# ScalarE's unused statistics outputs go to a scratch tile of 4-byte elements instead of the normalised tile of 2-byte elements

## The chip, the cores and the metric

One NeuronCore of one Trainium2 chip runs the kernel. The metric is the device time of one execution in microseconds (us); where several runs are compared, the median is quoted. The profile's own clock, the span, runs from the first to the last instruction and is about 1.8 us shorter than the device time (242.4 against 244.21 us for the profiled run of before). Of the engines, TensorE multiplies matrices, VectorE, ScalarE and GpSimd (POOL in the profile) do the elementwise work and the statistics, and SyncE issues most of the loads; a load "lands" when its data has arrived. The "granted clock" is TensorE's clock as a share of its full one, as the profile gives it. "Before" and "after" are the kernel without and with the change.

## The reference

It is one block of a diffusion transformer, with B=2, N=256 tokens, D=1152, two heads and an MLP of width F=4608, all in bf16:

```python
mod = (_silu(c) @ w_mod).reshape(B, 6, 1, D)
shift_a, scale_a, gate_a, shift_m, scale_m, gate_m = [mod[:, i] for i in range(6)]
h = _layernorm(x, axis=-1) * (1 + scale_a) + shift_a
qkv = (h @ wqkv).reshape(B, N, 3, H, Dh)
# ... q, k, v; softmax(q k^T / sqrt(Dh)) v, times wo
x = x + gate_a * a
h2 = _layernorm(x, axis=-1) * (1 + scale_m) + shift_m
m = _gelu(h2 @ w_fc1) @ w_fc2
return x + gate_m * m
```

Only the first layer norm matters here. Its mean and variance are taken per token over D.

## The kernel before

The 512 tokens lie in four token tiles of 128. The loads of x are issued first, on SyncE's queue, in the order 0, 1, 3, 2. Weight loads follow on the same queue: pieces of `w_scale_a` in turn with rows of `w_k`.

VectorE takes the statistics of tiles 1 and 3 with its own instructions. ScalarE takes those of tiles 0 and 2, each with two passes, Identity and Square. Each pass also gives the sum of its outputs (the trace has a read of an accumulator, 186 ns, after each), and only that sum is wanted; the call takes an output tile for the elements all the same. Before, they go into the tile that VectorE later fills with the normalised values.

```python
xns = [work.tile([P, D], BF16, name="xn", tag="xn", bufs=4) for _ in range(NT)]
# ...
def act_stats(t):
    for f, dst in ((ACT.Identity, dsum), (ACT.Square, dsq)):
        nc.scalar.activation(
            xns[t][:], x_sb[:, t, :], f, bias=x_sb[:, t, 0:1], scale=-1.0,
            accum_out=dst[:, t:t + 1],
        )
# ... the order in which the start is issued (cut):
warm(8, pwarm)                       # filler matmuls, meant to keep TensorE's clock up
act_stats(0)
act_stats(2)
for j in range(NPD):
    stats_piece(1, j)                # VectorE, tile 1
# ... variance and 1/std of tiles 0, 1 and 3
norm1(1, 0, CUT)                     # VectorE writes xns[1], xns[0]
norm1(0, 0, CUT)
pt_a = transpose_x([0, 1], BT[0])    # TensorE transposes xns[0], xns[1]
# ...
act_var(2)                           # needs the last ScalarE pass
nc.vector.tensor_scalar_mul(hT0[:, 0, 0:N], pt_a[:, 0, :], pm0[:, 0, 0:1])
# ... then matmuls with w_k, with scale_group(6, 8) and the like between:
def scale_group(k0, k1, tile_of=aux_tile):     # one block of scale_a = w_scale_a^T silu(c)
    # ...
            nc.tensor.matmul(
                pm[:, j - k0, :], w_scale_a[:, k, j * P:(j + 1) * P], sT[:, k, 0:B], # ...
            )
```

Much later the softmax's tile and then the residual x1 use one slot of scratch memory (the tag decides the slot):

```python
soft = act.tile([P, 4 * n_s * N], BF16, name="soft", tag="x1")
# ...
x1 = act.tile([P, NT, D], FP32, name="x1", tag="x1")
```

## Time and profile before

| | before |
|---|---|
| time, three runs | 243.87, 244.08, 244.36 us |
| span of the profiled run | 242.4 us |
| TensorE busy | 98% of the span |
| ScalarE busy | 25% of the span |
| the four statistics passes | 1254 to 1256 ns each |

First the profile page of before, part 1: busy time of each engine, its share of the span, and its count of instructions.

```profile
PE 237.1 (98%) x1701; PEld 145.0 (60%) x1701; DVE 91.4 (38%) x193; ACT 59.6 (25%) x120; POOL 28.9 (12%) x48
```

The chain of waits of before, in order of time (start, duration, what), from 8.5 us on:

```profile
8.53 2.51 SPq L104
11.04 0.04 issue
11.08 8.69 DMA w_scale_a<-in_w_mod_dram
19.77 0.05 issue
19.82 0.60 PE pm L245 x18
```

It is read backwards from the last instruction. From 19.82 us on nothing but TensorE holds the chain until the last output. Up to there this trace puts a weight load on it, and no ScalarE work. The `w_scale_a` piece in question is the fourth of five, and its matmuls belong to the blocks 6 and 7. I call it "the fourth piece". TensorE's own rows of the timeline show the wait (in brackets the idle time before an instruction and what ended it):

```profile
17.73 1.46 PE L278 MATMUL pk<-big,w_k 128*128 128x512 bf16 x6
19.82 0.60 PE L245 MATMUL pm<-sT,w_scale_a 128*128 128x2 bf16 x18 [0.64 <-DMA w_scale_a<-in_w_mod_dram]
```

The timeline of before, ScalarE only (start, duration, instruction, then in brackets the idle time before it and what ended it):

```profile
3.66 1.25 ACT L204 ACTIVATE xn<-x_sb 128x1152 bf16<-128x1152 bf16 x1
4.82 0.19 ACT L204 ACTIVATION_READ_ACCUMULATOR xn<-x_sb 128x1 f32 x1
5.04 1.25 ACT L204 ACTIVATE xn<-x_sb 128x1152 bf16<-128x1152 bf16 x1
...
7.18 1.26 ACT L204 ACTIVATE xn<-x_sb 128x1152 bf16<-128x1152 bf16 x1 [0.79 <-DMA x_sb<-in_x_dram]
...
8.56 1.26 ACT L204 ACTIVATE xn<-x_sb 128x1152 bf16<-128x1152 bf16 x1
```

From one pass to the next of the same tile is 1.38 us, which holds the pass and the read of its sum. The third pass waits for its token tile to arrive, not for a buffer. And the waits of before (who, for whom: us in total, times, longest):

```profile
PE pm L245 <- DMA w_scale_a<-in_w_mod_dram: 0.6, 1, 0.6
PEld L262 <- ACT xn L204: 0.6, 1, 0.6
```

The second line names ScalarE as what the first transposes waited for.

### The profile page before, as it was taken

The numbers are of one execution on the slowest core, as the hardware profiler recorded it, in microseconds if no ns is written. First come the engines' busy times: TensorE is split into PE (matmuls) and PEld (weight loads), VectorE is DVE, ScalarE is ACT, GpSimd is POOL, SyncE is SP. The second block draws the span as 40 slices with busy tenths as digits, with TensorE's granted clock in tenths as the row PEclk, the third lists the DMA queues.
The fourth block names the chain that finished last, engine by engine and source line by source line (L and its number), as shares of the span: only waits on it lengthen the run. The fifth ranks groups of instructions, "written<-read, shape, count | busy, mean of one in ns | idle before, by whom it ended". The sixth has DMA issues, their size and how long they took to land.

```text
span 242.4 us, 3999 instructions
## 1 busy us (share of the span) xinstructions
PE 237.1 (98%) x1701; PEld 145.0 (60%) x1701; DVE 91.4 (38%) x193; ACT 59.6 (25%) x120; POOL 28.9 (12%) x48
## 2 busy tenths in 40 slices
PE   8998999999999999999999999999999999999994
PEld 5675454465567665888854444444656656655674
DVE  4742442318416578831002999960010000000001
ACT  6622332307215032671422233322000000000000
POOL 2400000001400333200000000001121111111111
PEclk9999999999999999999999999999999999999999
DMA  6999999996499999239999999999300000000000
GB/s 184 325 317 318 376 366 391 390 392 236 107 314 398 388 374 145 40 62 351 390 391 392 342 327 290 271 326 286 97 16 16 20 16 16 20 16 17 29 22 16
DMA packets 48781, 53.29 MB, mean 220 GB/s; under 512 B 9587, under 2 KB 36475, under 8 KB 48763
## 3 DMA queue, kind: packets, MB, share of 16 engines
q1 hardware_dynamic: 41312, 50.14, 62.2%
q10 hardware_dynamic: 6939, 1.71, 5.1%
q0 software_dynamic: 512, 1.19, 1.8%
q8 instruction: 13, 0.21, 0.4%
q14 instruction: 5, 0.04, 0.1%
HBM read 50.14 MB, written 1.19 MB: 212 GB/s over the span
## 4 chain that ended last, share of the span: by engine, by line
PE 91%; SPq 4%; DMA 4%; issue 0%; DVE 0%; DVEq 0%
PE pacc L732 29%; PE pacc L788 29%; PE pacc L679 7%; PE pacc L588 7%; PE pq L510 7%; DMA w_scale_a<-in_w_mod_dram 4%; SPq L104 3%; PE pk L307 2%; PE pk L278 2%; PE pa L628 2%; PE ps_s L545 2%; PE pn L405 2%; SPq L86 1%; SPq L107 1%; PE pg L487 0%; PE pm L245 0%
## 5 line engine op out<-in xcount | busy, mean ns | idle before, releaser
L732 PE MATMUL pacc<-hT,w_f 128*128 128x256 bf16 (+1 forms) x432 | 70.5, 326 | 0.0
L788 PE MATMUL pacc<-w_f,gT 128*128 128x384 bf16 (+2 forms) x468 | 70.5, 314 | 0.0
L788 PEld LDWEIGHTS <-gT 128*128 128x128 bf16 x468 | 44.4, 98 | 26.3
L732 PEld LDWEIGHTS <-w_f 128*128 128x128 bf16 x432 | 42.2, 98 | 27.6
L794 DVE TENSOR_TENSOR tmp<-pacc,gate 128x384 f32<-128x384 f32 (+2 forms) x13 | 6.9, 527 | 65.6 <-PE pacc L788 57.2
L764 ACT ACTIVATE gT<-pacc 128x512 bf16<-128x512 f32 x24 | 14.3, 597 | 32.6 <-PE pacc L732 32.6
L458 DVE SCALAR_TENSOR_TENSOR part<-w_gate_m,s,part 128x1152 f32<-128x1152 bf16 x16 | 21.4, 1412 | 0.0
L796 POOL TENSOR_TENSOR o_sb<-tmp,x 128x384 bf16<-128x384 f32 (+1 forms) x12 | 11.7, 972 | 54.1 <-DVE tmp L794 54.1
L679 PE MATMUL pacc<-w_o,big 128*128 128x384 bf16 x108 | 17.9, 326 | 0.0
L510 PE MATMUL pq<-hT,w_q 128*128 128x512 bf16 x81 | 17.8, 379 | 0.0
L588 PE MATMUL pacc<-w_v,hT 128*128 128x384 bf16 x108 | 17.7, 326 | 0.0
L588 PEld LDWEIGHTS <-hT 128*128 128x128 bf16 x108 | 10.5, 98 | 7.1 <-issue 0.3
L679 PEld LDWEIGHTS <-big 128*128 128x128 bf16 x108 | 10.4, 98 | 7.2 <-issue 0.4
L510 PEld LDWEIGHTS <-w_q 128*128 128x128 bf16 x81 | 7.8, 97 | 9.5
L278 PE MATMUL pk<-big,w_k 128*128 128x256 bf16 (+1 forms) x72 | 13.2, 326 | 0.0
L685 POOL TENSOR_TENSOR x<-tmp,x_sb 128x384 f32<-128x384 f32 x8 | 7.3, 913 | 27.1 <-DMA w_scale_m<-in_w_mod_dram 15.2
L456 DVE TENSOR_SCALAR part<-w_gate_m,s 128x1152 f32<-128x1152 bf16 x2 | 1.6, 818 | 22.1 <-DMA w_gate_m<-in_w_mod_dram 22.1
L480 POOL DMA_DIRECT2D gates_dram<-nat_v x2 | 1.1, 536 | 67.7 <-DVE nat_v L478 67.7
L278 PEld LDWEIGHTS <-w_k 128*128 128x128 bf16 x72 | 6.7, 98 | 3.7 <-issue 0.3
L753 ACT ACTIVATE gT<-pacc 128x512 bf16<-128x512 f32 x12 | 6.5, 598 | 9.1 <-PE pacc L732 9.1
L173 PE MATMUL pwarm<-zeros 128*128 128x256 f32 x20 | 7.2, 527 | 1.2 <-DVE eps_t L93 1.2
L501 POOL DMA_DIRECT2D gates_dram<-nat x4 | 2.3, 586 | 50.6 <-DVE nat L498 49.9
(101 smaller groups left out, 165.9 us busy)
## 6 DMA issues: line engine op xcount, KB each, us to landing
w_f<-in_w_fc_dram SPq DMA_DIRECT2D x12, 864.0 KB, 14.6
w_f<-in_w_fc_dram SPq DMA_DIRECT2D x3, 1728.0 KB, 7.8
w_f<-in_w_fc_dram SPq DMA_DIRECT2D x2, 2592.0 KB, 17.2
w_gate_a<-in_w_mod_dram SPq DMA_DIRECT2D x3, 864.0 KB, 11.8
w_v<-in_wqkv_dram SPq DMA_DIRECT2D x3, 864.0 KB, 13.9
w_o<-in_wo_dram SPq DMA_DIRECT2D x3, 864.0 KB, 14.0
w_shift_m<-in_w_mod_dram SPq DMA_DIRECT2D x3, 864.0 KB, 8.6
w_scale_m<-in_w_mod_dram SPq DMA_DIRECT2D x3, 864.0 KB, 13.4
```

Source lines behind the costliest of these rows:

```text
L104: nc.sync.dma_start(w_k[:, k0:k1, c0:c1], wqkv_v[:, k0:k1, D + c0:D + c1])
L173: nc.tensor.matmul(dst[:, 0:T // 2], zeros32[:, 0:P], zeros32, start=True, stop=True)
L278: nc.tensor.matmul(pk[m][:, c0:c1], w_k[:, k, m * P:(m + 1) * P], hT0[:, k, c0:c1], start=(k == 0 and c0 == 0), stop=(k == KD - 1), skip_g ...
L458: nc.vector.scalar_tensor_tensor(part[:, b, :], wg[:, k, :], s32[:, k, b:b + 1], part[:, b, :], op0=ALU.mult, op1=ALU.add,)
L510: nc.tensor.matmul(pq[m][:], w_q[:, k, m * P:(m + 1) * P], hT[:, k, :], start=(k == 0), stop=(k == KD - 1), skip_group_check=True,)
L588: nc.tensor.matmul(pacc[:], hT[:, k, t * P:(t + 1) * P], w_v[:, k, pnl * PW:(pnl + 1) * PW], start=(k == 0), stop=(k == KD - 1),)
L679: nc.tensor.matmul(pacc[:], aT[:, k, t * P:(t + 1) * P], w_o[:, k, c0:c1], start=(k == 0), stop=(k == KD - 1),)
L685: (nc.gpsimd if pool_add else nc.vector).tensor_tensor(x1[:, t, c0:c1], tmp[:], x_sb[:, t, c0:c1], op=ALU.add)
L732: nc.tensor.matmul(dst, w_f1[m // KD][:, k, ml * P:(ml + 1) * P], hT[:, k, c0:c1], start=start, stop=(k == KD - 1), **kw,)
L764: nc.scalar.activation(gT[:, m, :], pacc[:], ACT.Gelu_apprx_tanh)
L788: nc.tensor.matmul(pacc[:], gT[:, kk, t * P:(t + 1) * P], w_f2[j][:, r, c0 - n * PW:c0 - n * PW + cw], start=(kk == 0), stop=(kk == KF - 1),)
L796: (nc.vector if last else nc.gpsimd).tensor_tensor(o_sb[:], tmp[:], x1[:, t, c0:c0 + cw], op=ALU.add)
```

## The change

The intent is that a write of a 2-byte element touches half a word, and a write of a 4-byte element a whole one. If half-word writes cost ScalarE time, then outputs that nobody reads should be written as whole words. The scratch for it lives in the slot that the softmax takes over later, so it needs no more memory.

```diff
+    sink = act.tile([P, D], FP32, name="sink", tag="x1")
+
     def act_stats(t):
         for f, dst in ((ACT.Identity, dsum), (ACT.Square, dsq)):
             nc.scalar.activation(
-                xns[t][:], x_sb[:, t, :], f, bias=x_sb[:, t, 0:1], scale=-1.0,
+                sink[:], x_sb[:, t, :], f, bias=x_sb[:, t, 0:1], scale=-1.0,
                 accum_out=dst[:, t:t + 1],
             )
```

## The prediction

> **What bounds the kernel now.** The page gives TensorE 98% of the 242.4 us span at full granted clock, ScalarE 25%. The chain of work that ended last is 91% TensorE; the rest lies almost wholly at its start. In order of time: SyncE's queue issues loads until 11.08 us, then a piece of w_scale_a lands at 19.77 us, and from 19.82 us the chain is TensorE without a break to 239.3 us. No ScalarE instruction is on it. In the table of stretches the DMA engines are 98% busy or more from 3 us on; TensorE is idle only 0.64 us between 12 and 24 us, just before 19.82 (the list of waits names that load). So weight loads bound the start, TensorE the rest.
>
> **What the change touches.** Four ScalarE activations (Identity and Square for token tiles 0 and 2), at 3.66, 5.04, 7.18 and 8.56 us, each 128x1152, bf16 in and out, 1254 to 1256 ns, each followed by a 186 ns accumulator read. Only the sums matter. Now the unused output is fp32 in a scratch tile instead of bf16 in xn.
>
> *Cost of the write.* The Trainium skill, "ScalarE: Activation LUTs", section "What ACT_TABLE_LOAD costs", gives 280 ns + 0.833 ns per element with a pointer bias, the same for fp32 and bf16: 1240 ns for 1152 elements. The trace has 1255 ns, so no half-word penalty is visible that could be removed. Other rows agree: the layer norm 2 activations (bf16 out) take 1349 ns at most for 1152 elements and 921 at least for 640, near 0.83 ns per element; softmax exponentials (256, fp32 out) take 485 ns, shift activations (256, bf16 out) 498 ns. I expect 1255 ns, within 20 ns, after the change.
>
> *Dependencies.* Removed: write-after-write between these activations and VectorE's normalisation into xn, and any wait of the transposes on ScalarE through xn. The normalisation needs the same activations' sums anyway (sum, variance, rstd), so it cannot start earlier. The trace puts a 0.56 us wait of the first transposes (8.60 us) on these activations, but VectorE's normalisation of that tile ended only at 8.49 us; at most about 0.1 us can come off there. Added: all four write one tile, but they already run in order on one engine. The softmax tile (first written at 56.0 us) and later x1 must follow the scratch, whose writes ended by 9.9 us, so no wait.
>
> **On the critical path.** Nothing. Even 0.1 us gained at 8.6 us, or some 0.5 us lost, runs into the w_scale_a load that lands at 19.77 us, for which TensorE already stands idle 0.64 us. No load waits for these tiles.
>
> **Prediction.** 244.1 us, range 243.6 to 244.6 (runs of before span 243.87 to 244.36). Faster by over 2%: 0.5%; within 2%: 99%; slower by over 2%: 0.5%.
>
> **What would show each step right or wrong.** Right: the four activations still 1255 ns, now 128x1152 f32 out; the first transposes at 8.5 to 8.6 us, waiting on VectorE; the wait for w_scale_a still ended at about 19.8 us, idle time before it the same or 0.1 us longer; softmax at 56 us with no new wait. Wrong: activations nearer 1.0 us (a half-word write did cost) or longer; a new wait in softmax or attention; the chain starting from ScalarE.
>
> **What would make it wrong.** Writes of fp32 slowing ScalarE by over 0.5 us before 12 us; the scratch shifting other tiles' addresses so that weight loads or matmuls change speed; a coarse release of the shared tag that holds up the softmax's DMA transposes.

## The result and the profile after

After: 243.53 us (median of 4 runs, 243.22 to 243.68). Before, with one run more: 243.98 us (4 runs, 243.50 to 244.36). The ratio is 0.9981 with a 95% interval of 0.996 to 1.0002. A ratio is the mean time of one kernel's fast runs over that of the other's of the same rounds, so it is not quite the ratio of the medians. The class "within 2%" came true; the median missed the predicted range by 0.07 us.

The program itself changed very little. A listing of both programs' instructions with their waits, line numbers aside, differs in three waits besides the four outputs: the first transposes no longer wait on ScalarE, a later transpose waits on the first ScalarE instruction (done at 3.6 us), and the third pass now also waits for the second, which runs before it on the same engine anyway.

Page of after, part 1:

```profile
PE 236.1 (98%) x1691; PEld 145.0 (60%) x1701; DVE 91.4 (38%) x193; ACT 59.8 (25%) x120; POOL 28.9 (12%) x48
```

(Ten matmul records are missing from this trace, as 1691 against 1701 weight loads shows. All ten are 512 columns wide, and their groups are 0.8 us less busy than before, so most of the 1.0 us of PE is not a saving.) The timeline of after, ScalarE only:

```profile
3.63 1.25 ACT L206 ACTIVATE sink<-x_sb 128x1152 f32<-128x1152 bf16 x1
4.79 0.19 ACT L206 ACTIVATION_READ_ACCUMULATOR sink<-x_sb 128x1 f32 x1
5.01 1.26 ACT L206 ACTIVATE sink<-x_sb 128x1152 f32<-128x1152 bf16 x1
...
6.68 1.26 ACT L206 ACTIVATE sink<-x_sb 128x1152 f32<-128x1152 bf16 x1 [0.32 <-DMA x_sb<-in_x_dram]
...
8.06 1.25 ACT L206 ACTIVATE sink<-x_sb 128x1152 f32<-128x1152 bf16 x1
```

The outputs are now f32, and nothing else about these rows has changed: still 1254 to 1256 ns each and 1.38 us from pass to pass. The third pass starts 0.50 us earlier only because the x tile landed earlier in this run. The change has no part in issuing that load, which goes out at the start and waits for nothing; whether the writes themselves could move loads is theory C below.

The chain of waits of after, the stretch that answers to the one above, and where it leaves TensorE late:

```profile
1.15 3.49 DMA x_sb<-in_x_dram
...
4.66 1.49 DVE stats L193 x3
...
17.85 1.29 PE pk L280 x6
19.14 0.43 PE pm L247 x18
...
93.45 3.74 DMA hT<-xn
...
97.29 0.36 DVE hT L653
```

In this run the fourth piece was there in time. TensorE takes it up at 18.98 us without a wait, where before had it at 19.82 us after 0.64 us of idling. The matmuls just ahead of it start at nearly the same time in both, 17.69 us here and 17.73 us before:

```profile
17.69 1.46 PE L280 MATMUL pk<-big,w_k 128*128 128x512 bf16 x6
18.98 0.59 PE L247 MATMUL pm<-sT,w_scale_a 128*128 128x2 bf16 x18
```

The chain at the start now runs through the x load and the statistics. So 0.84 us was gained at this point, nearly all of it by a load whose instructions the change does not touch. Then part of it went: the transposing DMA of the second layer norm was on the chain for 3.74 us and the first MLP matmul came at 97.69 us, 0.57 us ahead of before's 98.26 us. The span ended 0.5 us shorter.

The wait list of after has no line for `w_scale_a`. The first transposes now read:

```profile
PEld L264 <- DVE xn L233: 1.5, 2, 1.1
```

So the same wait has another name. Before, the listing of waits shows that these transposes waited for both VectorE and the third counted ScalarE instruction, which is the Square pass of tile 0. That pass ended at 6.4 us, its sum read included, more than two microseconds before the wait did. What really ended the wait at 8.60 us was VectorE's normalisation, done at 8.49 us.

### The profile page after: what moved, and what is told of

Its sections match the earlier page's. It is cut to its first block, busy times and chain, and to the rows that moved or that the text cites. A ratio compares the mean times of both kernels' runs of the same rounds, so it can differ in the third digit from the quotient of the medians.

```text
span 241.9 us, 3989 instructions
## 1 busy us (share of the span) xinstructions
PE 236.1 (98%) x1691; PEld 145.0 (60%) x1701; DVE 91.4 (38%) x193; ACT 59.8 (25%) x120; POOL 28.9 (12%) x48
## 4 chain that ended last, share of the span: by engine, by line
PE 91%; DMA 3%; DVE 3%; ACT 1%; issue 1%; SPq 0%; POOL 0%; DVEq 0%; ACTq 0%
PE pacc L790 29%; PE pacc L734 29%; PE pacc L590 7%; PE pq L512 7%; PE pk L280 5%; PE pacc L681 4%; PE pk L309 2%; PE pa L630 2%; PE ps_s L547 2%; DMA hT<-xn 2%; PE pn L407 2%; DMA x_sb<-in_x_dram 1%; DVE stats L193 1%; PE pt L264 1%; PE pm L247 1%
```

## The experiments

The first theory (A) is that the change itself does nothing and the 0.4 us is chance: when the x and weight loads land at the start differs from run to run. The rivals were B, that the change really saves about 0.4 us, either by the width or by the freed dependency; and later C, that the target of ScalarE's writes somehow moves the loads. A job's kernels run on one chip against shared runs of before.

### Before against itself (label before_again)

The edit is one comment. Expected:

> The kernel before under another name (one comment added), against itself: this measures the spread. Theory A (nothing in the change costs or saves; the 0.4 us between the medians is the spread of the weight loads' landing from run to run): ratio 1.000, but single runs from 243.2 to 244.4 us, and the profiled run shows a different landing time of the fourth w_scale_a piece (19.77 us in the first profile of before) with the span moving along. Theory B (the change really saves about 0.4 us): all runs of this kernel within 243.8 to 244.4 us, the landing again near 19.8 us with TensorE idle about 0.6 us before it.

Measured: 244.03 us (6 runs, 243.52 to 244.73) against 243.64 us for the same program's 11 shared runs; ratio 1.001, interval 0.9993 to 1.0027. The profiled run had the fourth piece late again: first matmul at 19.67 us after 0.47 us of idling. Theory B's band of 243.8 to 244.4 us is broken by before itself, on both sides.

### After once more (label after_again)

> The kernel after, five rounds. Theory A: ratio 0.999 to 1.001, interval holding 1; activations 1255 ns as before; the w_scale_a landing may be early or late. Theory B: ratio 0.998 with an interval below 1, and the w_scale_a piece again used without a wait at about 19.0 us.

Measured: 243.95 us (6 runs), ratio 1.0008, interval 0.9993 to 1.0024. The advantage of the first comparison is gone, though the trace again had no wait for the fourth piece (19.13 us). Theory A is right about the time. The passes took 1256 ns in the mean.

### Width alone (label half_words)

```diff
-    sink = act.tile([P, D], FP32, name="sink", tag="x1")
+    sink = act.tile([P, D], BF16, name="sink", tag="x1")
```

> The kernel after with the scratch as bf16: same tile slot, same addresses, same waits, only the width of the written elements is that of before. If the width does anything, this run parts from the kernel after: theory B-width says back to 244.0 us (ratio 1.000) while after has 0.998. Theory A: activations 1255 ns, ratio within 0.001 of that of after.

Measured: 243.54 us median. Five runs had 243.29 to 243.98 us at full clock, and one had 246.0 us with a mean granted clock of 0.992; with that one, the ratio is 1.0013, interval 0.998 to 1.0045. Three groups of ScalarE instructions by form, one each from before, after and this kernel, show what width costs (busy us, mean ns of one, idle before):

```profile
L204 ACT ACTIVATE xn<-x_sb 128x1152 bf16<-128x1152 bf16 x4 | 5.0, 1255 | 0.9 <-DMA x_sb<-in_x_dram 0.8
```

```profile
L206 ACT ACTIVATE sink<-x_sb 128x1152 f32<-128x1152 bf16 x4 | 5.0, 1255 | 0.4 <-DMA x_sb<-in_x_dram 0.3
```

```profile
L206 ACT ACTIVATE sink<-x_sb 128x1152 bf16<-128x1152 bf16 x4 | 5.0, 1255 | 0.8 <-DMA x_sb<-in_x_dram 0.6
```

So the width of the write costs nothing in the scratch tile, where both widths were run, and at two bytes the choice of tile costs nothing either. That the narrow scratch had the lowest median of the four kernels of this job, against the expectation of B, fits chance and not a word effect.

### A slot of its own (label own_slot)

```diff
-    sink = act.tile([P, D], FP32, name="sink", tag="x1")
+    sink = act.tile([P, D], FP32, name="sink", tag="sink")
```

> The kernel after with the fp32 scratch in a slot of its own, so that softmax and x1 have nothing to follow. Theory A: activations 1255 ns, softmax exponentials still first at 55 to 56 us, ratio within 0.001 of that of after. If the shared slot held anything up, this run is faster than after by more than 0.1%.

Measured: 243.82 us, ratio 1.0000, interval 0.9982 to 1.0018. Sharing the slot with the softmax shows no hold-up that this interval could tell from zero, and in the traces the softmax's first write comes no earlier with a slot of its own (55.3 us, against 55.1 us in after and 56.0 us in before).

### A third trace of before (label before_third)

After six traces there was a pattern that had to be tested: both traces of before had TensorE waiting for the fourth piece, and none of the four with the scratch had.

> A third trace of the kernel before, against itself. In the six traces so far the two of before have TensorE idle 0.47 and 0.64 us for the w_scale_a piece (matmuls from it start at 19.67 and 19.82 us), the four with the scratch have it at 18.9 to 19.2 us with 0.2 us of idle at most. Theory A (chance of the loads): the start of this stage in before can fall anywhere from 18.9 to 19.9 us; ratio 1.000 within 0.002. Theory C (where the activations write changes when the load lands, by a way that I can't name): 19.6 us or later again, idle 0.4 us or more.

Measured: 243.96 us, ratio 1.0018 with an interval of 1.0004 to 1.0032. That interval excludes 1 for one program against itself: even five rounds do not bring the error of such a ratio under 0.2%. In the trace the fourth piece was taken up at 19.46 us without a wait, and the chain of before now reads quite differently:

```profile
2.09 5.49 DMA x_sb<-in_x_dram
...
7.61 1.36 ACT xn L204 x2
8.96 0.03 issue
8.99 1.36 ACT xn L204 x2
...
10.37 0.16 DVE mv L222
10.53 0.28 DVE big L356
```

The x tile landed at 7.58 us, and both of ScalarE's passes over tile 2 are on the chain (x2 is a pass and the read of its sum). Theory C in the form that before always waits 0.4 us or more has fallen. The same program has either of two chains at its start, by which load is late. This trace is not the odd one: in those of half_words and own_slot the chain also runs through the load of that x tile and both of ScalarE's passes over it (from 7.07 and 7.31 us, 1.36 us each). In after_again it starts with the filler matmuls. So of the seven traces so far, three have ScalarE's statistics on the chain. My prediction that nothing of ScalarE's work lies on the path was therefore too strong.

| kernel | span, us | fourth piece first used, us | TensorE idle for it, us |
|---|---|---|---|
| before | 242.4 | 19.82 | 0.64 |
| before_again | 242.3 | 19.67 | 0.47 |
| before_third | 242.1 | 19.46 | 0 |
| after | 241.9 | 18.98 | 0 |
| after_again | 242.1 | 19.13 | 0 |
| half_words | 241.5 | 18.91 | 0 |
| own_slot | 241.8 | 19.16 | 0 |

### The wait taken away, in both kernels (labels before_no_wait, after_no_wait)

The last three blocks read a block that landed earlier, so the results are wrong.

```diff
-                    pm[:, j - k0, :], w_scale_a[:, k, j * P:(j + 1) * P], sT[:, k, 0:B],
+                    pm[:, j - k0, :], w_scale_a[:, k, min(j, 5) * P:(min(j, 5) + 1) * P], sT[:, k, 0:B],
```

> Before, with the matmuls of the last three w_scale_a blocks reading the block that landed before them (wrong result on purpose), so nothing waits for the piece that lands at 19.6 to 19.8 us. If the wait for that piece is what makes before's trace later, the stage starts at 18.9 to 19.1 us as in the traces with the scratch, the next load (w_k) may take over a part of the wait, and the total is 0 to 0.6 us lower: ratio 0.997 to 1.000.

> The same removal of the wait in the kernel after (wrong result on purpose). Theory A: the stage starts at 18.9 to 19.1 us, and the ratio is within 0.001 of that of before without the wait, as the change itself does nothing. Theory B (the change saves 0.4 us by itself): about 0.002 below that of before without the wait.

Measured: before without the wait 243.58 us (ratio 0.9996, interval 0.9981 to 1.001), after without it 243.66 us (1.0005, 0.9991 to 1.002), both against 243.70 us of before. Their traces take up the replaced block at 18.81 and 19.00 us. With the wait gone from both, the change still makes no difference, and the order is even the reverse of what B wants. It also says what the wait is worth on average, which is at most about 0.2% by the interval. Other chains stand right behind it: in these two traces the chain starts with VectorE's first work and its statistics (before_no_wait), and with the first `w_scale_a` piece, used from 9.25 us on (after_no_wait).

### One more pass (labels before_one_more, after_one_more, one_more_filled)

What is ScalarE's time at the start worth? One more Identity pass ahead of the last one, its sum into an unused column; the result stays correct.

```diff
-        for f, dst in ((ACT.Identity, dsum), (ACT.Square, dsq)):
+        for f, dst, col in ((ACT.Identity, dsum, t), (ACT.Identity, dsum, t + 1), (ACT.Square, dsq, t)):
+            if col > t and t == 0:
+                continue
             nc.scalar.activation(
                 xns[t][:], x_sb[:, t, :], f, bias=x_sb[:, t, 0:1], scale=-1.0,
-                accum_out=dst[:, t:t + 1],
+                accum_out=dst[:, col:col + 1],
             )
```

> Before, with one more of the four statistics activations (about 1.25 + 0.13 us, 1.38 us from start to start) ahead of the last one: result correct. It measures what ScalarE's time at the start is worth. Theory A with the slack that the first trace showed: the last activation ends 1.38 us later (near 11.2 us), 0.5 to 0.6 us vanish in the wait for w_scale_a, the rest shows: 0.7 to 1.4 us more, ratio 1.003 to 1.006. If ScalarE's statistics were wholly off the path, as I wrote in the prediction, ratio 1.000.

Measured: 245.62 us (244.68 to 246.68), ratio 1.0077, interval 1.0053 to 1.0102, so more than the pass itself in half of the runs. Three runs at a mean clock of 0.999 to 1.000 took 244.68, 244.75 and 245.25 us, 1.2 us over before (mean 244.89 less 243.70). Three at 0.991 to 0.992 took 246.00 to 246.68 us. The stretches of the profiled run, which was one of the latter, show it (stretch, length, busy us of PE, PEld, DVE, ACT and POOL with counts, granted clock, DMA share, GB/s):

```profile
8.00:10.00 2.00, 0.87 (x20) 0.69 (x20) 1.42 (x6) 1.97 (x3) 1.34 (x4) 1.00 1.12 339
10.00:12.00 2.00, 0.81 (x14) 0.41 (x12) 0.22 (x2) 1.89 (x6) 0.00 (x0) 1.00 1.17 310
12.00:14.00 2.00, 1.74 (x10) 1.30 (x10) 0.88 (x3) 0.52 (x3) 0.00 (x0) 0.55 1.15 319
14.00:16.00 2.00, 2.00 (x14) 1.47 (x13) 1.06 (x3) 0.47 (x1) 0.00 (x0) 0.60 1.13 326
```

TensorE waited 1.45 us for the later statistics,

```profile
12.26 1.44 PE L280 MATMUL pk<-big,w_k 128*128 128x256 bf16 x6 [1.45 <-DVE big L358]
```

and was busy less than half of the time from 8 to 12 us; then the granted clock was 0.50 from about 12.2 to 15.6 us. The Trainium skill, "TensorE: Matmul & The Clock Gate", section "Part 1: The HAM clock gate (the "warmup" mystery)", has this gate: half rate after an idle window of about 3.4 us, full rate again after a busy one, with windows that run free of the kernel. The length of the slow stretch here, 3.4 us, agrees with it, and so does that only some runs are hit. To see whether the gap is the cause, five filler matmuls more were put into it:

```diff
-    fill(1)
+    fill(6)
     k_step(0, 0, N)
```

> One more activation as before, with five more filler matmuls (128x512, 0.22 us each at full clock) in the gap where TensorE stood idle 1.45 us before the first w_k matmuls. In the run without them the granted clock fell to 0.50 from about 12.2 to 15.5 us, and three of its six runs with a mean clock of 0.991 to 0.992 took 246.0 to 246.7 us, the three others 244.7 to 245.3 us. If the idle gap brings the low clock: no run with a clock under 0.998, all at 244.6 to 245.3 us, ratio 1.004 to 1.006. If the low clock comes from something else: again some runs at 246 us.

Measured: 244.46 us, all six runs from 244.02 to 244.80 us at a clock of 0.999 or 1.000. The stretches of this run:

```profile
8.00:10.00 2.00, 1.51 (x28) 1.02 (x28) 1.08 (x4) 1.94 (x5) 1.09 (x3) 1.00 1.14 330
10.00:12.00 2.00, 1.62 (x11) 0.73 (x9) 0.66 (x3) 1.89 (x6) 0.00 (x0) 1.00 1.14 320
12.00:14.00 2.00, 2.00 (x20) 1.54 (x19) 1.42 (x5) 0.59 (x3) 0.00 (x0) 1.00 1.18 311
```

The low clock is gone, and with it the runs at 246 us: none of six, against three of six without the fillers. Loads also landed earlier in this trace (TensorE was busy 1.51 against 0.87 us from 8 to 10 us, where no filler was added), but that alone does not explain it: the trace of after_one_more below, without the fillers, reaches its first `w_k` matmuls earlier still (11.58 against 11.82 us), after a gap of 1.23 us, and its clock is 0.50 from about 12.0 to 15.4 us. The rise over before is smaller than I had written. This job's 11 runs of before contain two of 245.13 and 245.33 us with a clock of 0.993; against the nine others (mean 243.91 us) the filled kernel's mean of 244.44 us is 0.5 us more. (There is no trace of those two runs.) The ratio over all runs was 1.0009 (0.9983 to 1.0035) and the expected 1.004 to 1.006 was missed.

> The kernel after with one more activation. Theory A (the change alters no cost): as before with one more: full-clock runs 244.6 to 245.3 us, some at 0.992 and 246 to 246.7 us. If the whole-word write had made the activations cheaper or freed a wait, this would be less by what it saves.

Measured: 245.44 us (244.48 to 246.61), ratio 1.005, interval 1.0011 to 1.0089. Full-clock runs took 244.48, 244.72 and 244.88 us, the three others 246.01 to 246.61 us with 0.992 to 0.993. Both kernels with one more pass agree in both kinds of run, to 0.2 us of the means (244.69 against 244.89, and 246.38 against 246.26), on different chips. Against the full-clock runs of before in their own jobs the rises are 0.8 us in after and 1.2 us in before for the full-clock runs, and 2.5 and 2.6 us for the others. The 0.4 us between the first two rests on three runs each, with an error of near 0.3 us by my estimate from their spread, so it neither shows a saving nor excludes one of that size. One run, at 244.48 us, lies under the expected band.

### Shorter statistics, and both chains shorter (labels before_half_cols, before_both_short)

The passes over half of the columns; then that together with the wait taken away as above. Their outputs are wrong, which doesn't matter for the times.

```diff
-                xns[t][:], x_sb[:, t, :], f, bias=x_sb[:, t, 0:1], scale=-1.0,
+                xns[t][:, 0:D // 2], x_sb[:, t, 0:D // 2], f, bias=x_sb[:, t, 0:1], scale=-1.0,
```

> Before, with the four statistics activations over half of the columns (wrong result on purpose): each about 0.48 us shorter, the last one ends about 0.96 us earlier. Two-paths theory (the start is held by the later of two about equal chains: x load, ScalarE's statistics, normalisation, transposes; and the w_scale_a load): the load still lands at 18.7 to 19.8 us and takes the gain, TensorE's wait for it grows to 0.5 to 1.0 us, total 0 to 0.4 us lower, ratio 0.998 to 1.001. If ScalarE's chain alone set the start: 0.9 us lower, ratio 0.996.

> Half columns and no wait for the last w_scale_a pieces together (wrong result on purpose). Two-paths theory: with both chains shorter the stage starts earlier than in any run so far, about 18.0 to 18.5 us for the fourth block, unless the w_k load is next; total 0.5 to 0.9 us under before, ratio 0.996 to 0.998, clearly below each part alone.

Measured: 243.58 us (ratio 0.9973, interval 0.9947 to 0.9998) for half columns and 243.52 us (0.9972, 0.9946 to 0.9997) for both. The two slow-clock runs of before are in these ratios. Against its nine full-clock runs both gain about 0.4 us (means 243.55 and 243.53 against 243.91). So about 0.4 us of the 0.96 us that ScalarE gave back reached the total (from the spread of these runs I estimate a standard error near 0.2 us), and taking the wait away as well added nothing that can be seen. That contradicts my expectation of 0.5 to 0.9 us for both, clearly below each part alone; the ratio of 0.9972 lies in the band of 0.996 to 0.998 only through those two slow-clock runs. In the trace of half columns the chain starts with the fourth piece, landing at 19.30 us: with ScalarE's passes shorter, that load is last again. The trace of both together gives one reason for its own run: its chain begins with yet another load, the first `w_scale_a` piece, which landed at 9.85 us,

```profile
2.57 7.28 DMA w_scale_a<-in_w_mod_dram
9.85 0.05 issue
9.89 0.62 PE pm L245 x18
```

so there are at least three chains, not two, that can be last. The traces are too few to say how often each of them is.

## Why the prediction was right or wrong

- **Width of the write: right.** 1254 to 1256 ns were predicted unchanged and measured unchanged, in three combinations of tile and width. The Trainium skill, "ScalarE: Activation LUTs", section "What ACT_TABLE_LOAD costs", gives 280 ns and 0.833 ns per element for a pass whose bias comes from a tile, for fp32 and bf16 alike, which makes 1240 ns for this shape as an estimate; the traces have 1255.
- **Dependencies: right in effect.** The freed wait on ScalarE had been satisfied two microseconds before it mattered, and the up to 0.1 us I allowed there did not come: the transposes started at 8.80 us after against 8.60 us before, since VectorE's first tile landed later. The shared slot held nothing up (own_slot 1.0000).
- **"On the critical path. Nothing": wrong as a general statement.** It held for the one trace I had. In another trace of the same kernel, and in those of half_words and own_slot, both passes of tile 2, with their sums' reads, are on the chain, and in the full-clock runs one more pass cost 1.2 us of its 1.38 us (in after, in another job, 0.8 us: 244.69 less 243.91). "some 0.5 us lost, runs into the w_scale_a load" is thereby not to be counted on either, nor is "the wait for w_scale_a still ended at about 19.8 us": in after the piece was taken up at 18.98 us without a wait. This did no harm to the forecast only because the passes did not change; that much was luck.
- **The range: wrong, and this is the step that failed.** "range 243.6 to 244.6 (runs of before span 243.87 to 244.36)" took three runs for the spread and their middle for the centre. Over all jobs, 46 full-clock runs of before (four of them without a clock on record) lie from 243.25 to 244.75 us, with a mean of 243.88, a median of 243.83 and a standard deviation of 0.36 us; 11 of them are under 243.6 us. The centre was 0.27 us too high (244.1 against 243.83), and the lower end of the range lay only 0.23 us under that median. The ten runs of after have a mean of 243.79 us, 0.09 us (0.04%) from before. So before itself could have missed the range: of random draws of four among those 46 runs, I estimate that about 9 in 100 have a median under 243.6 us. That this draw was one of them is chance; that the range left no room for it is the error.

What stays open: an effect of the change under about 0.2% could not be told from chance here, since one kernel against itself gave 1.001 and 1.0018. The wait for the fourth piece was absent in all four traces with a scratch and in one of three of before; no mechanism for a link is visible in the programs and the totals show none. The other traces speak against one without excluding it: the slowest `w_scale_a` piece took 8.2 to 8.7 us from issue to landing in three of the eight traces whose passes write into xn, but 7.4 to 7.7 us in the other five, as in the six with a scratch (7.3 to 7.5 us). By chance alone all three would fall on those eight in about one case of seven (an estimate from these counts). Why a load lands at one time in one run and 0.5 us later in another was not tested.

## What to carry to other kernels

Before changing the width or the target of an output nobody reads, compare rows of the same operation with narrow and wide outputs in the trace: if they already take equal time, the width has nothing to give on that engine. A chain of waits from one trace is one draw; where several loads and a short computation finish within a microsecond of each other, take more traces before calling work off the path. And measure the kernel against itself before writing a range: three close runs can understate the spread.

## What the Trainium skill lacked or had wrong

- "TensorE: Matmul & The Clock Gate" asks for no idle gaps over about 3 us to keep the clock. Here the longest gap was 1.45 us, with TensorE busy 1.66 of the 3.4 us from 8.8 to 12.2 us, and the granted clock still fell to 0.50 for 3.4 us in that run (in after_one_more, after a gap of 1.23 us, the same); three of six runs of each of these kernels had a mean clock of 0.991 to 0.993. In the traced run with the fillers, busy 1.51 and 1.62 us in each 2 us, it did not fall, and none of its six runs had a mean clock under 0.999. The page mentions frequent short idle times as a second cause, but does not say how much of a window may be idle.
- The same page says that the number of slow matmuls at a kernel's start varies from run to run, but not that the mean clock of a kernel that mostly runs at full clock can drop in a few of its runs: 2 of 11 runs of before in one job, at a mean clock of 0.993 and 245.13 and 245.33 us, against 243.25 to 244.75 us for the others. Where in those two runs the clock fell is not known, as neither was traced.
- "ScalarE: Activation LUTs" gives no time for the read of an accumulated sum: a separate instruction of 186 ns after each pass, 1.38 us from pass to pass with 1.255 us for the pass.
